# A seventh unit's long rows turned by way of DRAM, and a new hand-laid order

## Chip, cores and metric

The kernel runs on one core of one Trainium2 chip. The metric is device time in microseconds (us): the median of three runs was 361.75 us (361.44 to 361.85).

## What is computed

Two attention layers follow each other, in float32. The first is attention over a window of 128 positions with 4 sink positions (batch 4, 8 heads, 768 positions, head width 64); its output, seen as `x` with 512 columns, enters a mixture of four attention experts, of which each position takes the best two.

```python
scores = where(is_sink | in_window, scale * q @ k.T, -1e9)
x      = softmax(scores) @ v                      # per batch and head, then heads side by side
logits = x @ w_gate;  w = softmax of the two largest logits
for e in range(4):                                # causal attention of expert e, width 64
    a   = softmax(causal(scale * (x @ wq[e]) @ (x @ wk[e]).T))
    out += weight_of(e) * (a @ (x @ wv[e]) @ wo[e])
```

## The kernel before

The work is cut into 24 units. A unit of the first layer is one batch and one pair of heads; a unit of the second layer is one batch and one pair of experts. Units are named by three digits, batch, pair, layer: unit 001 is batch 0, expert pair 0, second layer. They come in the order of `ORD` and `LAST` (L1944, L1945): the four head pairs of batch 0, then 110, 100, **001**, 120, 130, 011, 210 and so on; 301 and 311 are the last.

A unit of the second layer (`second`, L1828) projects `x` to queries and keys, then works six blocks of 128 rows (`wide_rows`, L1566). Row block i sees i+1 key blocks. Scores go to PSUM (L1385), DVE takes the mask and the minimum (L1602), ACT the exponential and its sum (L1610), POOL and DVE make the factor, ACT or POOL scale the row (L1256, L1258). The values can only be applied (L1424) once the row is transposed, and there are two ways to do that:

- **On PE** (`transposed`, L1463, and `turned`, L1453): every 128 by 128 block is transposed by two matmuls against a unit matrix (L1457) into PSUM, and ACT or DVE carry it back to SBUF (`pt`, L1247 and L1249). Rows 4 and 5 are cut in two parts (`SPLIT`, L1942), each with its own transposing step and its own step of applying values.
- **By way of DRAM** (`by_way_of_dram`, L1536): the row is scaled into a tile `u`, DVE transposes the 32 by 32 squares within it (two instructions, L1547), one DMA writes `u` to the DRAM tile `there` (L1550), four DMAs read it back with the squares exchanged (L1554), and PE applies the values straight from `u` in one step (L1424). PE transposes nothing. There are three `u` tiles and four `there` tiles (L1043).

`AWAY` (L1940) says which rows of which units go by way of DRAM: rows 3, 4 and 5 of the units 011, 101, 111, 201, 211 and 301. A unit with such rows also takes its row pairs from the last to the first (`groups[::-1]` in `wide_rows`). Units 001 and 311 have none.

The order of every instruction on every engine is fixed while the program is built. `Plan.emit` (L907) simulates the engines with a cost per step and picks, again and again, the next step. On PE the choice goes by one key (L958): the step's priority, plus a charge `STAY` (and a term with `BULK`) where the step needs another shape of the PE array than the last, plus `HURRY` per 100 ns of waiting. The dictionary `NUDGE` adds a number of its own to the priority of single steps and kinds of steps (3,033 entries), and `ONLY` fixes for 396 steps which engine takes them. Shapes of the array are FULL (128 by 128), "cols" (128 rows by 64 columns: applying values), "rows" (64 by 128: scores and PE transposes) and "quad" (64 by 64: banded scores). Where PE would have nothing to do in the first 130 us, dummy matmuls are put in (L1057). On the chip each engine runs its list in order and waits on semaphores.

Of the kernel before, what the change touches and what calls it, by code (L numbers as in the profile page):

```python
# [34 lines left out]
for other in ("ROWS", "FULL", "cols", "rows"):  # L35
# [10 lines left out]
    "busy_PE": 2.7, " ": -0.4, " busy_PE": 50.2, " busy_PE 0": 4.1, "sink_values_DVE": 20.3, " sink_values_DVE": 16.0,  # L46
    " sink_values_DVE 0": -121.8, "load_SP": -59.6, " load_SP": 21.7, " load_SP 0": 11.3, "again_SP": 5.1,
    " again_SP": 21.0, " again_SP 0": -23.8, "sink_values_ACT": -3.5, " sink_values_ACT": -29.8, " sink_values_ACT 0": 49.4,
    "sink_values_POOL": 12.3, " sink_values_POOL": 5.5, " sink_values_POOL 0": -91.6, "sink_values_SP": 4.4,
    " sink_values_SP": 35.9, " sink_values_SP 0": -24.8, "load_SPACT": 0.1, " load_SPACT": 12.9, " load_SPACT 0": -10.8,  # L50
# [768 lines left out]
    "311 store_SPACT 3": SP, "311 fn_DVEACT 20": ACT, "311 fn_DVEACT 21": DVE, "311 store_SPACT 5": SP,  # L819
}  # L820

HURRY = 71.82
STAY = 104.82
BULK = -0.39
# [1197 lines left out]
```

## Time and profile before

| | before |
|---|---|
| median of 3 runs | 361.75 us |
| the profiled execution's own time | 361.39 us |
| its span, first to last instruction | 359.7 us |
| granted TensorE clock, mean | 0.998 of full |
| matmuls / DVE / ACT / POOL busy | 98% / 81% / 77% / 51% of the span |

The profile is one execution. Busy time of an engine is the union of its instructions; matmuls overlap and their ends are modelled, so their start times are the safer reading. "PEld" is the loading of weights into the array, which runs beside matmuls. In the chain of waits the trace is followed back from the last instruction to whatever released it.

### The profile page before, as it was taken

To read this page: it belongs to the slowest core of one execution; us is meant where nothing else is said; L and a number is where in the kernel's file an instruction comes from. 1 tells how busy PE (TensorE), PEld (TensorE's weight loads), DVE (VectorE), ACT (ScalarE), POOL (GpSimd) and SP (SyncE) were. 2 spreads that over 40 slices of the span, in tenths; PEclk is the share of its full clock that TensorE was granted. 3 is DMA by queue.
4 is the path that set the end of the run, shared out by engine and by line. 5 is a ranking of instruction groups with operands and counts; after the bars stand their busy time and mean duration, and the time that the engine had idled before them with its cause. 6 is when DMAs were issued, how large, how long until landed. Compare 5 with 4: busy or idle time off the path is not lost.

```text
span 359.7 us, 13333 instructions
## 1 busy us (share of the span) xinstructions
PE 351.2 (98%) x4822; PEld 307.1 (85%) x4822; DVE 290.6 (81%) x1263; ACT 278.7 (77%) x985; POOL 183.2 (51%) x432
## 2 busy tenths in 40 slices
PE   8989999999999999999999999999999999999995
PEld 7877789998888889978888888978898889988884
DVE  4899989599979979649799987489699875587951
ACT  2899999299998899758898977489899956056931
POOL 4298999778276764334646550153558600150420
PEclk9999999999999999999999999999999999999999
DMA  7877787943550798329787595029800463059313
GB/s 200 214 178 144 149 165 142 173 77 84 92 87 3 234 263 156 58 88 307 207 159 124 162 283 122 11 87 352 218 7 4 145 223 76 14 201 300 103 58 118
DMA packets 130849, 52.05 MB, mean 145 GB/s; under 512 B 109728, under 2 KB 125088, under 8 KB 130784
## 3 DMA queue, kind: packets, MB, share of 16 engines
q1 hardware_dynamic: 118336, 46.23, 52.0%
q10 hardware_dynamic: 12448, 4.98, 5.3%
...
## 4 chain that ended last, share of the span: by engine, by line
PE 80%; ACT 7%; DMA 4%; DVE 3%; POOL 3%; issue 2%; SPq 0%; ACTq 0%; POOLq 0%; DVEq 0%
PE b L1424 19%; PE b L1839 17%; PE b L1913 10%; PE b L1866 9%; PE b L1385 8%; PE b L1457 7%; PE b L1398 5%; PE b L1380 2%; DMA u<-there 2%; ACT p L1610 2%; PE b L1924 1%; ACT p L1740 1%; DMA there<-u 1%; PE b L1428 1%; DMA vn<-in_v_dram 1%
## 5 line engine op out<-in xcount | busy, mean ns | idle before, releaser
L1610 ACT ACTIVATE p<-p,st 128x256 f32<-128x256 f32 (+5 forms) x96 | 63.6, 665 | 9.8 <-DVE st L1602 9.6
L1740 ACT ACTIVATE p<-p,st 128x132 f32<-128x132 f32 x128 | 51.3, 406 | 3.2 <-DVE st L1736 3.1
L1602 DVE CUSTOM_DVE_ANT_0 p<-b,cmask 128x384 f32<-128x384 f32 (+3 forms) x96 | 45.7, 502 | 1.9 <-PE b L1385 1.5
L1247 ACT ACTIVATE pt<-b 128x256 f32<-128x256 f32 (+3 forms) x101 | 38.5, 419 | 7.5 <-PE b L1457 7.3
L1385 PE MATMUL b<-ks,qs 64*128 64x384 f32 (+3 forms) x384 | 42.2, 338 | 0.0
L1424 PE MATMUL b<-pt,vn 128*64 128x128 f32 x448 | 39.0, 280 | 0.3 <-ACT pt L1247 0.3
L1866 PE MATMUL b<-wvh,x 128*128 128x260 f32 x192 | 36.9, 285 | 0.0
L1440 POOL TENSOR_TENSOR st<-st 128x2 f32<-128x2 f32 (+1 forms) x47 | 9.3, 197 | 52.7 <-ACT p L1610 36.1
L1457 PE MATMUL b<-ident,p 64*128 64x64 f32 x760 | 36.0, 226 | 0.0
L1457 PEld LDWEIGHTS b<-ident,p 64*128 64x128 f32 x760 | 30.4, 138 | 5.4 <-issue 2.5
L1385 PEld LDWEIGHTS b<-ks,qs 64*128 64x128 f32 x384 | 31.6, 186 | 3.3 <-issue 0.7
L1839 PE MATMUL b<-x,wqh 128*128 128x256 f32 (+1 forms) x128 | 32.8, 343 | 0.0
L1839 PE MATMUL b<-x,wkh 128*128 128x256 f32 (+1 forms) x128 | 32.5, 340 | 0.0
L1913 PE MATMUL b<-woh,y 128*128 128x512 f32 x96 | 32.2, 402 | 0.0
L1753 POOL TENSOR_TENSOR p<-p,st 128x528 f32<-128x528 f32 x23 | 24.5, 1066 | 15.0 <-DVE st L1445 10.8
L1547 DVE STREAM_TRANSPOSE u<-u 128x640 f32<-128x640 f32 (+2 forms) x36 | 28.5, 824 | 4.0 <-ACT u L1256 3.7
L1736 DVE CUSTOM_DVE_ANT_0 p<-b,pair_mask 128x132 f32<-128x132 f32 x128 | 31.6, 286 | 0.1
L1679 ACT ACTIVATE p<-p,st 128x256 f32<-128x256 f32 (+1 forms) x64 | 29.1, 460 | 2.9 <-DVE st L1674 2.8
L1866 PEld LDWEIGHTS b<-wvh,x 128*128 128x128 f32 x192 | 30.4, 188 | 0.7 <-issue 0.3
L1249 DVE COPY pt<-b 128x256 f32<-128x256 f32 (+3 forms) x63 | 27.5, 453 | 2.6 <-PE b L1457 2.5
L1424 PEld LDWEIGHTS b<-pt,vn 128*64 128x64 f32 x448 | 25.1, 136 | 4.6 <-issue 1.7
L1866 PE MATMUL b<-wvl,x 128*128 128x260 f32 x96 | 27.1, 282 | 0.0
...
## 6 DMA issues: line engine op xcount, KB each, us to landing
vn<-in_v_dram SPq DMA_DIRECT2D x24, 192.0 KB, 3.3
...
there<-u SPq DMA_DIRECT2D x6, 768.0 KB, 4.8
u<-there SPq DMA_DIRECT2D x24, 192.0 KB, 4.6
...
```

The lines of the kernel that those rows point to most:

```text
L1247: nc.scalar.activation(dst(), src(), AF.Copy)
L1385: nc.tensor.matmul(o, self.qs.t[hs, a, qs], keys(hs, b), start=n == 0, stop=n == 2)
L1424: nc.tensor.matmul(o[e * 64:e * 64 + 64], lhs, rhs, start=e not in self.begun, stop=last and self.done == len(self.steps))
L1457: nc.tensor.transpose(t[g].t[:, n, :], x[gs], ident[gs, gs])
L1602: nc.vector.tensor_tensor_reduce(out=one(e)[:, cs], in0=s2[e].t[:, :(c1 - c0) * 128], in1=mask(c0, c1), scale=times, scalar=st.t[:, 3, es] ...
L1610: nc.scalar.activation(x, x, AF.Exp, bias=st.t[:, 0, es], scale=-1.0, accum_out=st.t[:, 1, es])
L1679: nc.scalar.activation(x, x, AF.Exp, bias=st.t[:, 0, n:n + 1], scale=-1.0, accum_out=st.t[:, 1, n:n + 1])
L1736: nc.vector.tensor_tensor_reduce(out=p.t[:, n, :], in0=s2[e].t[:, 248 * r:248 * r + SW], in1=pair_mask, scale=-scale, scalar=BIG, op0=OP.a ...
L1740: nc.scalar.activation(p.t[:, n, :], p.t[:, n, :], AF.Exp, bias=st.t[:, 0, n:n + 1], scale=-1.0, accum_out=st.t[:, 1, n:n + 1])
L1839: nc.tensor.matmul(t.t, w[a][:, c, es], X[b, c].t[:, x, cs], start=c == 0 and m == 0, stop=c == NCH - 1 and m == 2)
L1866: nc.tensor.matmul(t.t[:, :VW], X[b, c].t[:, a, qs], W["wv"][w][:, c, :], start=c == 0 and n == 0, stop=c == NCH - 1 and n == 2)
L1913: nc.tensor.matmul(t.t, Y[b, c].t[:, a, qs], W["wo"][w][:, c, :], start=c == 0 and n == 0, stop=c == EP - 1 and n == 2)
```

## The change

Unit 001 is added to `AWAY`: its rows 3, 4 and 5 go by way of DRAM, and its row pairs are taken from the last to the first. The three constants of PE's key change, and `NUDGE` and `ONLY` are replaced throughout (3,069 and 430 entries; of the 2,942 nudges that both have, three keep their value). Nothing else differs.

```diff
-    "001 tr_PE 4": 0.5, "001 fn_DVEACT 14": 26.1, "001 fn_DVEACT 15": 30.9, "001 all_of_PE 3": -1.9, "001 tr_PE 5": 23.7,
...
+    "001 turn_DVE 3": 82.4, "001 by_way_of_dram_SP 1": 186.4, "001 back_SP 1": -0.2, "001 av_PE 1": -12.8,
...
-HURRY = 71.82
-STAY = 104.82
-BULK = -0.39
+HURRY = 80.98
+STAY = 193.1
+BULK = -55.63
...
-    AWAY, MOVE = {u: (3,4,5) for u in ((0, 1), (1, 0), (1, 1), (2, 0), (2, 1), (3, 0))}, 250
+    AWAY, MOVE = {u: (3,4,5) for u in ((0, 0), (0, 1), (1, 0), (1, 1), (2, 0), (2, 1), (3, 0))}, 250
```

## Rows read from the trace of the kernel before

**Rows 1.** The page's table of busy time: microseconds, share of the span, instructions.
```profile
PE 351.2 (98%) x4822; PEld 307.1 (85%) x4822; DVE 290.6 (81%) x1263; ACT 278.7 (77%) x985; POOL 183.2 (51%) x432
```

**Rows 2.** Who PE's matmuls waited for over the whole span: microseconds in total, times, longest; five rows of 0.6 us or less follow. Asked for the stretch from 60 us to the end alone, the view has the second of these rows and no other.
```profile
PE b L1924 <- DVE lanes L1110: 1.1, 1, 1.1
PE b L1424 <- DMA u<-there: 0.8, 1, 0.8
PE b L1398 <- POOL kx L1322: 0.7, 1, 0.7
```

**Rows 3.** Busy time by stretch: the stretch in us, its length, then PE, PEld, DVE, ACT and POOL busy (instructions), granted clock, DMA share, GB/s.
```profile
0.00:20.00 20.00, 18.38 (x402) 15.70 (x404) 14.19 (x84) 11.18 (x45) 8.56 (x32) 1.00 0.83 215
...
80.00:100.00 20.00, 20.00 (x342) 17.48 (x341) 19.50 (x98) 19.69 (x69) 10.69 (x23) 1.00 0.50 92
100.00:120.00 20.00, 19.97 (x268) 17.50 (x268) 17.88 (x61) 18.02 (x66) 15.59 (x37) 1.00 0.36 82
120.00:140.00 20.00, 20.00 (x292) 17.65 (x289) 17.74 (x88) 18.32 (x76) 11.65 (x29) 1.00 0.88 217
```

**Rows 4.** PE's instructions in order of time while unit 001 works its rows: start us, us, then line, operation, tiles, shape and count.
```profile
74.18 0.60 PE L1385 MATMUL b<-ks,qs 64*128 64x256 f32 x6
...
86.60 0.71 PE L1457 MATMUL b<-ident,p 64*128 64x64 f32 x16
87.15 0.87 PE L1380 MATMUL b<-kx,qn 64*128 64x128 f32 x8
87.86 0.53 PE L1457 MATMUL b<-ident,p 64*128 64x64 f32 x12
88.32 1.58 PE L1398 MATMUL b<-kx,qn 64*64 64x196 f32 x48
89.83 0.59 PE L1457 MATMUL b<-ident,p 64*128 64x64 f32 x12
90.25 0.87 PE L1380 MATMUL b<-kx,qn 64*128 64x128 f32 x8
91.06 2.40 PE L1424 MATMUL b<-pt,v 128*64 128x128 f32 x40
93.39 1.41 PE L1457 MATMUL b<-ident,p 64*128 64x64 f32 x32
```

**Rows 5.** Pieces of the chain of waits, followed back from the end of the stretch 70 to 120 us: start us, us, engine, tile, line, count. L1457 transposes, L1424 applies values.
```profile
78.12 0.46 PE b L1457 x10
...
91.12 2.33 PE b L1424 x40
...
107.00 1.17 PE b L1457 x32
110.16 0.81 PE b L1424 x12
```

**Rows 6.** Groups of instructions by form over the whole span (count, busy us, mean ns of one): the squares' transposes on DVE, the copies out of PSUM, the scaling of rows.
```profile
L1547 DVE STREAM_TRANSPOSE u<-u 128x768 f32<-128x768 f32 x12 | 11.1, 951 | 0.9 <-ACT u L1256 0.9
L1547 DVE STREAM_TRANSPOSE u<-u 128x640 f32<-128x640 f32 x12 | 9.7, 828 | 2.5 <-ACT u L1256 2.5
L1547 DVE STREAM_TRANSPOSE u<-u 128x512 f32<-128x512 f32 x12 | 8.1, 692 | 0.6 <-POOL u L1258 0.3 <-ACT u L1256 0.3
...
L1247 ACT ACTIVATE pt<-b 128x384 f32<-128x384 f32 x37 | 17.0, 496 | 5.1 <-PE b L1457 4.9
L1247 ACT ACTIVATE pt<-b 128x512 f32<-128x512 f32 x3 | 1.7, 596 | 0.0
...
L1258 POOL TENSOR_SCALAR u<-p,st 128x640 f32<-128x640 f32 x11 | 8.8, 800 | 0.1
L1258 POOL TENSOR_SCALAR p<-p,st 128x640 f32<-128x640 f32 x2 | 1.6, 800 | 0.2
```

**Rows 7.** DMA issues by tile: issuing queue, count, KB each, median us from issue to landing.
```profile
there<-u SPq DMA_DIRECT2D x6, 768.0 KB, 4.8
u<-there SPq DMA_DIRECT2D x24, 192.0 KB, 4.6
...
there<-u SPq DMA_DIRECT2D x6, 512.0 KB, 5.1
u<-there SPq DMA_DIRECT2D x24, 128.0 KB, 4.7
```

**Rows 8.** The tile `there`: its DMA instructions (ns to issue one, min/median/max, first and last start), and the time to landing of all of them.
```profile
L1554 SPq DMA_DIRECT2D u<-there x72: 302/430/1563, 123.4 to 332.1; - x72
L1550 SPq DMA_DIRECT2D there<-u x18: 326/344/1114, 116.9 to 324.0; - x18
...
DMA to landing us min/median/max: 2.5/4.5/7.1
```

**Rows 9.** The chain of waits around 205 us, where it leaves PE: start us, us, what.
```profile
206.24 4.16 DMA there<-u
...
211.84 7.06 DMA u<-there
...
219.04 1.53 PE b L1424 x24
```

**Rows 10.** SP's issues in the stretch 80 to 120 us, in order of time: the first and the last of the four lines that load queries and keys of units to come (sixteen DMAs in all).
```profile
89.98 2.04 SPq L1804 DMA_DIRECT2D qn<-in_q_dram  x4
...
101.51 2.54 SPq L1804 DMA_DIRECT2D kn<-in_k_dram  x4
```

More of the change, by code (lines that the diff above doesn't have):

```diff
@@ L45 @@
 NUDGE = {
[L46 to L50, printed above, removed]
@@ L817 @@
[L817 to L824 removed]
+    " load_SPACT 1": SP, " load_SPACT 2": ACT, " load_SPACT 4": ACT, " load_SPACT 6": SP, "000 load_SPACT 0": SP,
+    "000 load_SPACT 1": SP, "000 load_SPACT 3": SP, "000 load_SPACT 4": SP, "000 fn_DVEACT 1": DVE, "000 fn_DVEACT 6": ACT,
@@ new lines @@
+    "000 fn_DVEACT 7": DVE, "000 total_DVEPOOL 0": DVE, "000 norm_POOLACT 0": ACT, "000 norm_POOLACT 1": POOL,
+    "000 fn_DVEACT 8": ACT, "000 fn_DVEACT 9": ACT, "000 norm_POOLACT 2": ACT, "000 fn_DVEACT 10": DVE,
+    "000 fn_DVEACT 11": ACT, "000 fn_DVEACT 12": DVE, "000 fn_DVEACT 13": ACT, "000 fn_DVEACT 14": ACT,
+    "000 fn_DVEACT 15": DVE, "000 fn_DVEACT 16": ACT, "010 load_SPACT 0": SP, "010 load_SPACT 1": SP,
+    "010 fn_DVEACT 0": DVE, "010 fn_DVEACT 1": DVE, "010 fn_DVEACT 2": ACT, "010 fn_DVEACT 3": DVE, "010 fn_DVEACT 4": DVE,
@@ new lines @@
+    "010 fn_DVEACT 5": ACT, "010 fn_DVEACT 6": DVE, "010 fn_DVEACT 7": DVE, "010 norm_POOLACT 0": ACT,
+    "010 norm_POOLACT 1": POOL, "010 fn_DVEACT 8": ACT, "010 fn_DVEACT 9": DVE, "010 norm_POOLACT 2": ACT,
+    "010 fn_DVEACT 10": DVE, "010 fn_DVEACT 11": DVE, "010 fn_DVEACT 12": DVE, "010 fn_DVEACT 13": ACT,
+    "010 total_DVEPOOL 2": DVE, "010 norm_POOLACT 3": POOL, "010 fn_DVEACT 14": ACT, "010 fn_DVEACT 15": DVE,
+    "010 fn_DVEACT 16": ACT, "010 fn_DVEACT 17": DVE, "020 load_SPACT 0": SP, "020 load_SPACT 1": SP,
@@ new lines @@
+    "030 fn_DVEACT 7": ACT, "030 total_DVEPOOL 0": DVE, "030 norm_POOLACT 1": POOL, "030 fn_DVEACT 8": DVE,
+    "030 total_DVEPOOL 1": POOL, "030 norm_POOLACT 2": ACT, "030 fn_DVEACT 11": DVE, "030 total_DVEPOOL 2": POOL,
+    "030 fn_DVEACT 14": DVE, "110 load_SPACT 0": SP, "110 load_SPACT 2": SP, "110 total_DVEPOOL 0": DVE,
+    "110 norm_POOLACT 0": POOL, "110 norm_POOLACT 1": ACT, "110 fn_DVEACT 4": ACT, "110 norm_POOLACT 3": ACT,
+    "110 fn_DVEACT 8": ACT, "110 fn_DVEACT 9": DVE, "100 load_SPACT 1": SP, "100 load_SPACT 2": SP,
@@ new lines @@
+    "100 total_DVEPOOL 0": DVE, "100 norm_POOLACT 0": ACT, "100 fn_DVEACT 1": ACT, "100 total_DVEPOOL 1": POOL,
+    "100 fn_DVEACT 2": DVE, "100 fn_DVEACT 3": ACT, "100 fn_DVEACT 4": ACT, "100 total_DVEPOOL 2": POOL,
+    "100 norm_POOLACT 3": POOL, "100 fn_DVEACT 8": DVE, "100 fn_DVEACT 9": ACT, "001 fn_DVEACT 0": DVE,
+    "001 fn_DVEACT 1": ACT, "001 fn_DVEACT 5": DVE, "001 norm_POOLACT 0": POOL, "001 total_DVEPOOL 1": POOL,
+    "001 norm_POOLACT 2": ACT, "001 norm_POOLACT 3": POOL, "001 total_DVEPOOL 2": DVE, "001 norm_POOLACT 4": POOL,
@@ new lines @@
+    "001 fn_DVEACT 6": ACT, "001 total_DVEPOOL 3": POOL, "001 norm_POOLACT 7": POOL, "001 total_DVEPOOL 4": DVE,
+    "001 norm_POOLACT 8": POOL, "001 norm_POOLACT 9": POOL, "001 fn_DVEACT 8": DVE, "001 fn_DVEACT 9": ACT,
+    "001 norm_POOLACT 11": ACT, "001 fn_DVEACT 10": ACT, "120 load_SPACT 1": SP, "120 load_SPACT 2": SP,
+    "120 norm_POOLACT 0": ACT, "120 norm_POOLACT 1": POOL, "120 fn_DVEACT 1": ACT, "120 norm_POOLACT 2": POOL,
+    "120 fn_DVEACT 2": ACT, "120 fn_DVEACT 4": DVE, "120 fn_DVEACT 5": DVE, "120 total_DVEPOOL 2": POOL,
@@ new lines @@
+    "120 fn_DVEACT 6": DVE, "120 fn_DVEACT 8": DVE, "120 fn_DVEACT 9": DVE, "130 load_SPACT 0": SP, "130 load_SPACT 1": SP,
+    "130 total_DVEPOOL 0": DVE, "130 norm_POOLACT 0": ACT, "130 norm_POOLACT 1": ACT, "130 fn_DVEACT 1": ACT,
+    "130 norm_POOLACT 2": POOL, "130 fn_DVEACT 2": ACT, "130 fn_DVEACT 4": ACT, "130 fn_DVEACT 5": ACT,
+    "130 total_DVEPOOL 2": DVE, "130 fn_DVEACT 6": ACT, "130 fn_DVEACT 8": ACT, "130 fn_DVEACT 9": ACT,
+    "011 total_DVEPOOL 0": POOL, "011 norm_POOLACT 0": POOL, "011 total_DVEPOOL 1": POOL, "011 norm_POOLACT 2": POOL,
@@ new lines @@
+    "011 norm_POOLACT 3": POOL, "011 total_DVEPOOL 2": POOL, "011 norm_POOLACT 4": POOL, "011 norm_POOLACT 5": POOL,
+    "011 fn_DVEACT 0": ACT, "011 total_DVEPOOL 3": POOL, "011 norm_POOLACT 6": POOL, "011 total_DVEPOOL 4": POOL,
+    "011 norm_POOLACT 9": POOL, "011 fn_DVEACT 2": ACT, "011 norm_POOLACT 10": ACT, "011 norm_POOLACT 11": POOL,
+    "011 fn_DVEACT 5": DVE, "011 store_SPACT 0": ACT, "011 fn_DVEACT 7": DVE, "011 store_SPACT 1": SP,
+    "011 fn_DVEACT 8": ACT, "011 fn_DVEACT 9": DVE, "011 store_SPACT 3": SP, "011 fn_DVEACT 10": DVE,
@@ new lines @@
+    "011 store_SPACT 5": ACT, "210 load_SPACT 1": SP, "210 load_SPACT 2": SP, "210 norm_POOLACT 0": POOL,
+    "210 norm_POOLACT 1": POOL, "210 fn_DVEACT 0": ACT, "210 total_DVEPOOL 1": POOL, "210 norm_POOLACT 2": POOL,
+    "210 norm_POOLACT 3": ACT, "210 fn_DVEACT 6": DVE, "210 fn_DVEACT 7": DVE, "210 fn_DVEACT 8": ACT,
+    "200 load_SPACT 0": SP, "200 load_SPACT 2": SP, "200 norm_POOLACT 0": POOL, "200 norm_POOLACT 1": POOL,
+    "200 fn_DVEACT 0": DVE, "200 fn_DVEACT 1": ACT, "200 total_DVEPOOL 1": POOL, "200 norm_POOLACT 2": ACT,
@@ new lines @@
+    "101 norm_POOLACT 10": POOL, "101 norm_POOLACT 11": POOL, "101 fn_DVEACT 10": ACT, "101 fn_DVEACT 11": ACT,
+    "220 load_SPACT 0": SP, "220 total_DVEPOOL 0": DVE, "220 norm_POOLACT 1": POOL, "220 fn_DVEACT 0": DVE,
+    "220 fn_DVEACT 1": ACT, "220 total_DVEPOOL 1": POOL, "220 fn_DVEACT 2": DVE, "220 fn_DVEACT 3": ACT,
+    "220 fn_DVEACT 4": DVE, "220 fn_DVEACT 5": DVE, "220 norm_POOLACT 3": ACT, "220 fn_DVEACT 8": ACT,
+    "220 fn_DVEACT 9": ACT, "230 load_SPACT 1": SP, "230 fn_DVEACT 0": ACT, "230 fn_DVEACT 1": ACT,
@@ new lines @@
+    "230 total_DVEPOOL 1": POOL, "230 fn_DVEACT 2": ACT, "230 fn_DVEACT 3": ACT, "230 fn_DVEACT 4": ACT,
+    "230 fn_DVEACT 5": DVE, "230 total_DVEPOOL 2": POOL, "230 norm_POOLACT 3": POOL, "230 fn_DVEACT 7": ACT,
+    "230 fn_DVEACT 8": ACT, "111 total_DVEPOOL 0": POOL, "111 norm_POOLACT 0": POOL, "111 norm_POOLACT 1": POOL,
+    "111 total_DVEPOOL 1": DVE, "111 norm_POOLACT 3": POOL, "111 norm_POOLACT 4": POOL, "111 total_DVEPOOL 3": DVE,
+    "111 norm_POOLACT 6": ACT, "111 norm_POOLACT 7": POOL, "111 total_DVEPOOL 4": POOL, "111 norm_POOLACT 8": ACT,
@@ new lines @@
+    "111 fn_DVEACT 2": ACT, "111 fn_DVEACT 3": DVE, "111 total_DVEPOOL 5": DVE, "111 norm_POOLACT 11": POOL,
+    "111 fn_DVEACT 4": ACT, "111 fn_DVEACT 5": ACT, "111 store_SPACT 0": SP, "111 fn_DVEACT 7": ACT,
+    "111 store_SPACT 1": SP, "111 fn_DVEACT 8": DVE, "111 store_SPACT 2": SP, "111 store_SPACT 3": SP,
+    "111 fn_DVEACT 10": ACT, "111 store_SPACT 4": SP, "111 fn_DVEACT 11": ACT, "111 store_SPACT 5": ACT,
+    "300 load_SPACT 0": SP, "300 load_SPACT 1": SP, "300 total_DVEPOOL 0": POOL, "300 norm_POOLACT 0": POOL,
@@ new lines @@
+    "201 fn_DVEACT 6": ACT, "201 norm_POOLACT 7": ACT, "201 total_DVEPOOL 4": DVE, "201 norm_POOLACT 9": POOL,
+    "201 fn_DVEACT 8": ACT, "201 fn_DVEACT 9": ACT, "201 total_DVEPOOL 5": DVE, "201 norm_POOLACT 10": ACT,
+    "201 norm_POOLACT 11": ACT, "201 fn_DVEACT 10": ACT, "310 load_SPACT 0": SP, "310 total_DVEPOOL 0": DVE,
+    "310 norm_POOLACT 0": POOL, "310 total_DVEPOOL 1": POOL, "310 norm_POOLACT 2": POOL, "310 fn_DVEACT 2": DVE,
+    "310 fn_DVEACT 3": ACT, "310 fn_DVEACT 4": ACT, "310 fn_DVEACT 5": DVE, "310 total_DVEPOOL 2": DVE,
@@ new lines @@
+    "310 norm_POOLACT 3": POOL, "310 fn_DVEACT 6": DVE, "310 fn_DVEACT 8": DVE, "320 load_SPACT 0": SP,
+    "320 load_SPACT 1": SP, "320 norm_POOLACT 0": POOL, "320 fn_DVEACT 0": ACT, "320 fn_DVEACT 1": ACT,
+    "320 total_DVEPOOL 1": POOL, "320 norm_POOLACT 2": POOL, "320 fn_DVEACT 3": DVE, "320 fn_DVEACT 4": ACT,
+    "320 norm_POOLACT 3": POOL, "320 fn_DVEACT 6": DVE, "320 fn_DVEACT 7": ACT, "320 fn_DVEACT 8": DVE,
+    "320 fn_DVEACT 9": DVE, "330 load_SPACT 1": SP, "330 total_DVEPOOL 0": POOL, "330 norm_POOLACT 1": ACT,
@@ new lines @@
+    "330 fn_DVEACT 0": ACT, "330 fn_DVEACT 1": DVE, "330 total_DVEPOOL 1": DVE, "330 norm_POOLACT 2": POOL,
+    "330 fn_DVEACT 2": DVE, "330 fn_DVEACT 3": ACT, "330 fn_DVEACT 4": DVE, "330 fn_DVEACT 5": DVE,
+    "330 norm_POOLACT 3": POOL, "330 fn_DVEACT 7": ACT, "330 fn_DVEACT 8": ACT, "330 fn_DVEACT 9": ACT,
+    "211 norm_POOLACT 1": POOL, "211 total_DVEPOOL 1": DVE, "211 norm_POOLACT 2": POOL, "211 norm_POOLACT 3": POOL,
+    "211 total_DVEPOOL 2": DVE, "211 norm_POOLACT 4": ACT, "211 norm_POOLACT 5": POOL, "211 fn_DVEACT 0": DVE,
@@ new lines @@
+    "211 fn_DVEACT 1": ACT, "211 norm_POOLACT 7": POOL, "211 total_DVEPOOL 4": POOL, "211 norm_POOLACT 8": POOL,
+    "211 norm_POOLACT 9": ACT, "211 fn_DVEACT 2": ACT, "211 total_DVEPOOL 5": POOL, "211 norm_POOLACT 11": POOL,
+    "211 fn_DVEACT 4": ACT, "211 fn_DVEACT 5": ACT, "211 fn_DVEACT 6": ACT, "211 fn_DVEACT 7": ACT, "211 store_SPACT 1": SP,
+    "211 fn_DVEACT 11": ACT, "211 store_SPACT 5": SP, "301 fn_DVEACT 0": DVE, "301 fn_DVEACT 1": ACT,
+    "301 fn_DVEACT 2": DVE, "301 fn_DVEACT 3": ACT, "301 fn_DVEACT 4": ACT, "301 total_DVEPOOL 0": DVE,
@@ new lines @@
+    "311 norm_POOLACT 0": POOL, "311 fn_DVEACT 0": DVE, "311 fn_DVEACT 1": DVE, "311 total_DVEPOOL 1": DVE,
+    "311 norm_POOLACT 2": POOL, "311 norm_POOLACT 3": POOL, "311 fn_DVEACT 2": ACT, "311 fn_DVEACT 3": DVE,
+    "311 fn_DVEACT 5": ACT, "311 total_DVEPOOL 3": POOL, "311 fn_DVEACT 6": DVE, "311 total_DVEPOOL 4": DVE,
+    "311 norm_POOLACT 8": POOL, "311 fn_DVEACT 8": ACT, "311 fn_DVEACT 9": DVE, "311 fn_DVEACT 10": ACT,
+    "311 fn_DVEACT 11": DVE, "311 total_DVEPOOL 5": DVE, "311 norm_POOLACT 11": POOL, "311 fn_DVEACT 12": ACT,
@@ L825 @@
+    "311 fn_DVEACT 13": DVE, "311 fn_DVEACT 15": ACT, "311 fn_DVEACT 16": DVE, "311 store_SPACT 0": SP,
+    "311 store_SPACT 1": ACT, "311 store_SPACT 2": SP, "311 fn_DVEACT 19": ACT, "311 store_SPACT 3": SP,
+    "311 fn_DVEACT 20": ACT, "311 store_SPACT 4": ACT, "311 fn_DVEACT 21": ACT, "311 store_SPACT 5": SP,
+}
+HURRY = 80.98
+STAY = 193.1
+BULK = -55.63
 FILL_COST, FILL_KEEP, FILL_END = 220.0, 0.0, 130000.0
```

132 lines of the change are left out of this document (34 added, 98 removed), and 1339 rows, old and new, of the table NUDGE.

## Prediction

> **What bounds the kernel.** I read the table of busy time first: PE 98% [rows 1]. Since the ends of matmuls are modelled, that alone proves nothing, so I went on to what PE waited for. In the whole span that is a handful of waits near 1 us or below, and from 60 us on a single one, 0.8 us for a read back from DRAM [rows 2]. The stretches agree: 18.38 us of matmuls in the first 20 us, then 20.00, 19.97 and 20.00 of 20 from 80 to 140 us, at full clock [rows 3]. So from 60 us to the end PE's list of instructions is the time. What leaves this list shortens the kernel one for one, as long as no other engine takes its place. The nearest is DVE: 19.50 and 17.88 us busy of 20 in the two stretches in which unit 001 works its rows, ACT 19.69 and 18.02 [rows 3].
>
> The Trainium skill's page "Perfetto Trace Analysis", section "Identifying the Most-Contended Engine", warns that matmul busy time is a poor measure of headroom and wants the busy share of weight loads instead; that is 85% here. By it 15% of the engine would be free and the sum below would be nothing (a rival). The waits speak against it: PE hardly waits for anyone.
>
> **What leaves PE.** Row 3 has 4 key blocks, row 4 has 5, row 5 has 6; each block is two heads by two halves, so 16 + 20 + 24 = 60 transposes go. The chain's pieces give their price without the modelled ends [rows 5]: 10 transposes take 0.46 us and 32 take 1.17, so one is (1.17 - 0.46) / 22 = 0.032 us, and a run of them costs 0.46 - 0.32 = 0.14 us besides, the turn of the array to another shape. 60 x 0.032 = **1.94 us**.
>
> The 60 stand in five steps (one for row 3, two each for rows 4 and 5). In time order they are the runs of 16, 12, 12 and 32, the last holding other transposes too [rows 4]. I let four runs disappear: 4 x 0.14 = **0.55 us**. Bounds: none, if other transposes move in, and about 1.4 us, if all five go and each also joins its two neighbours into one run.
>
> Applying the values is the same number of matmuls from `u` as from `pt`. But five steps become three. A run of 12 takes 0.81 us and one of 40 takes 2.33 [rows 5], so a matmul is 0.054 us and the run itself 0.16. Two runs fewer would be 0.32 us; half of it, as such runs are often joined already: **0.16 us** (bounds 0 and 0.32). Together 2.65 us, between 1.9 and 3.7.
>
> **What it adds elsewhere, and why I cost it at nothing.**
> - DVE gets two transposes of squares per row: 2 x (0.69 + 0.83 + 0.95) = 4.94 us [rows 6]. It loses its share of ten copies out of PSUM, which at ACT's means would be 0.60 us for 512 columns and 0.50 for 384; most of them are ACT's today, so ACT gains about 4 us and DVE pays nearly all of its 4.94. From 80 to 120 us DVE has 40 - 37.4 = 2.6 us free [rows 3]. That is not enough unless the order gives ACT other copies, which it can: every such copy may go to either engine, and the new `ONLY` redistributes them. The cover is thus ACT's freed time. Bounds: 0, and 4.94 - 2.6 = 2.3 us. I take 0, since together the two engines gain as much as they lose.
> - Scaling a row into `u` costs what scaling it in place costs: 800 ns each for 640 columns [rows 6].
> - SP issues three writes and twelve reads: 3 x 0.34 + 12 x 0.43 = 6.2 us [rows 8], and the reads wait on SP until the write has landed, 3.4 to 5.1 us by size at the median [rows 7]. Behind them stand loads of later units [rows 10]: sixteen DMAs from 90 to 104 us, which now share the queue. DVE needs them for its turns; they are prefetched, and a few us of delay is covered. If not, DVE stands still, and this falls into the first rival.
> - Data: 768 + 640 + 512 KB out and the same back, 3.84 MB more in a stretch that moves 92 and 82 GB/s at DMA shares of 0.50 and 0.36. The stretch after it, with detours of its own, carries 217 GB/s at 0.88 [rows 3]; the extra 96 GB/s over 40 us fits.
> - The unit's row pairs come from the last to the first, so its first scores need all projections. Before, its first long scores began at 74.18 us, behind the projections as well [rows 4]; nothing is lost.
>
> Here a rule of the Trainium skill speaks against the change. "DMA: Bandwidth & Descriptors", section "Rules for kernel authors", puts transposing by a plain DMA with a rearranged pattern at 19 times the cost of the hardware's DMA transpose. The rows do not show such a penalty: a read back of 192 KB lands in 4.6 us at the median, a plain write of 768 KB in 4.8 [rows 7]. Were the four reads of row 5 to take 19 times the 4.8, some 91 us by my estimate, PE would wait for most of it.
>
> **What the new order brings.** Every other instruction may move, and the trace shows none of that, so I bound it. To the good: the one late read back costs PE 0.8 us [rows 2], from a write of 4.16 us and a read of 7.06 us in sequence [rows 9]; and turns of the array. From 86.60 to 93.39 us PE begins nine runs of one shape [rows 4], at 0.14 to 0.16 us each. In the key the charge for a turn rises from 104.82 / 71.82 = 1.46 to 193.1 / 80.98 = 2.38 hundred ns of waiting, so fewer turns are chosen where nudges do not decide. If over some 200 us of such stretches one run in twelve went, that is about 200 x 9 / 6.8 / 12 x 0.15 = 3.3 us. To the bad: the same number of turns more, 3.3 us, or new waits. I take the value nearest to a row, the 0.8 us wait and one turn of 0.16: **1.0 us** gained, ends -4.1 and +3.3.
>
> **The sum.** 361.39 us of the profiled execution - 2.65 - 1.0 = 357.7. The median stands 0.36 us above that execution, so 358.1 us for the median. The good end is 361.75 - 3.7 - 4.1 = 354.0; the bad side is the rivals'.
>
> **Rivals.**
> - *DVE takes PE's place* between 80 and 120 us. For it: the 2.3 us that do not fit. Against it: ACT's freed time, and that PE has work of other units to do meanwhile. Price: 2.3 us and the order's 1.0 not had: 358.1 + 3.3 = 361.4 us, at worst; a milder form lies near 360.
> - *The reads back land after PE has come to their matmuls* (slower). PE's list is fixed; where the data is not there, everything behind waits. Before, one of 18 rows was late, by 0.8 us [rows 2]. After, 21 rows stand at new places, and landings spread from 2.5 to 7.1 us around 4.5 [rows 8]. If a third, seven rows, came late by as much: 7 x 0.85 = 6.0 us, so 361.75 - 2.65 + 6.0 = 365.1 us. It decides from the fifth late row on (4.3 x 0.85 = 3.65 us, all that I forecast). Against it: 17 of 18 were in time, and the new detours lie where DMA has most room.
> - *PE is not the bound*: the weight loads' 85% are the truth, the transposes ran beside other work, and nothing changes: 361.7 us. Against it: waits after 60 us are 0.8 us in all, and the pieces of the chain grow linearly with the count.
> - *The order saves far more*, over 4.1 us of turns and waits: below 354.0 us.
>
> That the change doesn't do what it says I exclude: `second` looks up exactly this key in `AWAY`.
>
> **Chances.** Forecast 0.61; DVE 0.15; late reads 0.16; not the bound 0.03; far more 0.05. About 0.2% (0.7 us) is what a measurement of this kernel can tell from no change. Faster by more than that: 0.61 + 0.05 + two thirds of DVE's 0.15 = 0.76. Within it: the other third, "not the bound", and a little of the late reads: 0.09. Slower: 0.15. The range is 354.0 to 362.0 us; it leaves out the 0.05 below and nearly all of the late reads above.
>
> **What would show it.** In the changed kernel's profile: 700 transposes in the group at L1457 where there were 760, 42 transposes of squares where there were 36, 21 writes to `there`; in PE's waits still no more than about 1 us after 60 us; DVE under 20 us of 20 in 80 to 120 us. If the forecast is wrong, PE's busy time falls while waits for `u` or DVE grow by as much (second and first rival), or PE's runs become more and shorter. Wrong by size would be an order that saves whole microseconds of turns.

## The result, and the profile after

The changed kernel took **364.32 us** at the median (360.78 to 367.67, 20 runs) against 361.44 us of the kernel before on the same chip: the ratio is 1.007 [1.0048, 1.0093], so it is slower by 0.7%, where 358.1 us and a gain were forecast. The ratio leaves out executions in the slower state, two of these twenty. Its profiled execution took 362.49 us, with a span of 360.8. Lines of the changed kernel are 22 higher than before: transposes on PE L1479, values L1446, squares on DVE L1569, loads L1826.

The table of busy time, against [rows 1]:

```profile
PE 352.1 (98%) x4802; PEld 307.9 (85%) x4802; DVE 292.0 (81%) x1272; ACT 271.3 (75%) x952; POOL 190.6 (53%) x449
```

20 matmuls are missing, not 60: the sixty transposes went, and there are 40 more dummy matmuls (118, before 78), nearly all of them in the first 40 us. DVE gained 1.4 us, ACT lost 7.4, and POOL gained 7.4: work did move between them.

The groups of instructions by form, against [rows 5, 6], and the tile `there`, against [rows 8]. The change does what it says:

```profile
L1479 PE MATMUL b<-ident,p 64*128 64x64 f32 x700 | 34.4, 226 | 0.0
...
L1569 DVE STREAM_TRANSPOSE u<-u 128x768 f32<-128x768 f32 x14 | 13.1, 958 | 0.2 <-POOL u L1280 0.2
L1569 DVE STREAM_TRANSPOSE u<-u 128x640 f32<-128x640 f32 x14 | 11.4, 830 | 1.1 <-ACT u L1278 1.1
L1569 DVE STREAM_TRANSPOSE u<-u 128x512 f32<-128x512 f32 x14 | 9.6, 696 | 0.5 <-POOL u L1280 0.4
```

```profile
L1576 SPq DMA_DIRECT2D u<-there x84: 302/431/1447, 87.8 to 333.0; - x84
L1572 SPq DMA_DIRECT2D there<-u x21: 319/343/348, 83.8 to 324.9; - x21
...
DMA to landing us min/median/max: 2.4/4.4/7.2
```

Who PE waited for in the changed kernel (total us, times, longest), against [rows 2]:

```profile
PE b L1450 <- DVE ks L1332: 1.2, 1, 1.2
PE b L1946 <- DVE lanes L1132: 1.1, 1, 1.1
PE b L1446 <- DMA u<-there: 1.1, 1, 1.1
```

The middle one stands at the beginning, as before. The other two are new. The stretches, in the columns of [rows 3], show where:

```profile
80.00:100.00 20.00, 20.00 (x240) 16.62 (x240) 18.52 (x82) 19.56 (x74) 14.65 (x33) 1.00 0.73 197
100.00:120.00 20.00, 18.93 (x333) 16.95 (x324) 19.50 (x85) 17.07 (x61) 12.86 (x29) 1.00 0.82 169
160.00:180.00 20.00, 20.00 (x223) 16.95 (x223) 16.02 (x61) 13.18 (x48) 9.45 (x22) 1.00 0.88 262
180.00:200.00 20.00, 18.55 (x324) 16.26 (x320) 19.21 (x84) 18.55 (x71) 14.05 (x34) 1.00 0.63 118
```

PE is 1.07 us short in the stretch 100 to 120, and 1.45 us in 180 to 200. The first is the read back of unit 001's row 5, the new detour. The second comes from ACT. In ACT's order of time (start, us, engine, line, what) the four query loads of unit 330 are issued at 171.27 us, and ACT does nothing else for 5 us:

```profile
171.24 0.22 ACT L1269 ACTIVATE sk<-b 64x64 fp32r<-64x64 f32 x1
171.27 5.13 ACTq L1826 DMA_DIRECT2D qn<-in_q_dram  x4
176.45 0.41 ACT L1762 ACTIVATE p<-p,st 128x132 f32<-128x132 f32 x1 [4.99 <-DVE kx L1377]
```

In the kernel before, ACT issued the same four loads at 221.77 us in 0.34 + 1.69 us:

```profile
221.77 0.34 ACTq L1804 DMA_DIRECT2D qn<-in_q_dram  x1
222.16 1.69 ACTq L1804 DMA_DIRECT2D qn<-in_q_dram  x3
```

In the changed kernel ACT's later work shifts, the turn of the queries and the split of the keys on DVE come late, and PE waits at 182 us.

### The profile page after: what moved, and what is told of

Same layout as the page of the kernel before. It is cut to its first block, busy times and chain, and to the rows that moved or that the text cites. A ratio compares the mean times of both kernels' runs of the same rounds, so it can differ in the third digit from the quotient of the medians.

```text
span 360.8 us, 13315 instructions
## 1 busy us (share of the span) xinstructions
PE 352.1 (98%) x4802; PEld 307.9 (85%) x4802; DVE 292.0 (81%) x1272; ACT 271.3 (75%) x952; POOL 190.6 (53%) x449
## 4 chain that ended last, share of the span: by engine, by line
PE 74%; DVE 10%; DMA 5%; SPq 4%; ACT 3%; issue 2%; POOL 1%; DVEq 0%; POOLq 0%; ACTq 0%
PE b L1446 18%; PE b L1861 13%; PE b L1407 9%; PE b L1888 8%; PE b L1935 7%; PE b L1479 7%; PE b L1420 5%; DMA u<-there 2%; PE b L1402 2%; SPq L1826 2%; PE b L1359 1%; DVE kx L1377 1%; PE b L1946 1%; PE b L1450 1%; DVE u L1569 1%
## 5 line engine op out<-in xcount | busy, mean ns | idle before, releaser
L1632 ACT ACTIVATE p<-p,st 128x768 f32<-128x768 f32 (+5 forms) x96 | 63.7, 666 | 9.2 <-DVE st L1624 9.0
L1407 PE MATMUL b<-ks,qs 64*128 64x384 f32 (+3 forms) x384 | 43.5, 340 | 0.2 <-DVE ks L1332 0.2
L1269 ACT ACTIVATE pt<-b 128x256 f32<-128x256 f32 (+3 forms) x96 | 36.5, 416 | 7.2 <-PE b L1479 4.8
L1446 PE MATMUL b<-pt,vn 128*64 128x128 f32 x448 | 39.2, 279 | 0.0
L1569 DVE STREAM_TRANSPOSE u<-u 128x640 f32<-128x640 f32 (+2 forms) x42 | 34.0, 828 | 1.7 <-ACT u L1278 1.1
L1479 PE MATMUL b<-ident,p 64*128 64x64 f32 x700 | 34.4, 226 | 0.0
L1462 POOL TENSOR_TENSOR st<-st 128x2 f32<-128x2 f32 (+1 forms) x53 | 10.5, 199 | 43.5 <-ACT p L1632 24.1
L1479 PEld LDWEIGHTS b<-ident,p 64*128 64x128 f32 x700 | 28.8, 138 | 5.2 <-issue 2.0
L1861 PE MATMUL b<-x,wkh 128*128 128x512 f32 (+1 forms) x128 | 32.3, 340 | 0.0
L1446 PEld LDWEIGHTS b<-pt,vn 128*64 128x64 f32 x448 | 25.5, 136 | 2.9 <-DVE st L1624 0.3
L1471 POOL TENSOR_TENSOR st<-st,gate 128x2 f32<-128x2 f32 x48 | 9.2, 197 | 35.4 <-DVE st L1467 29.5
L1446 PE MATMUL b<-u,v 128*64 128x128 f32 x420 | 26.2, 274 | 1.1 <-DMA u<-there 1.1
```

Source lines behind the costliest of these rows:

```text
L1269: nc.scalar.activation(dst(), src(), AF.Copy)
L1407: nc.tensor.matmul(o, self.qs.t[hs, a, qs], keys(hs, b), start=n == 0, stop=n == 2)
L1446: nc.tensor.matmul(o[e * 64:e * 64 + 64], lhs, rhs, start=e not in self.begun, stop=last and self.done == len(self.steps))
L1479: nc.tensor.transpose(t[g].t[:, n, :], x[gs], ident[gs, gs])
L1569: nc.vector.transpose(x(), x())
L1632: nc.scalar.activation(x, x, AF.Exp, bias=st.t[:, 0, es], scale=-1.0, accum_out=st.t[:, 1, es])
```

## Experiments

All kernels with a list EDITS replay the planned order of the kernel they start from, with single steps moved or given to another queue just before the instructions are made; nothing else differs, and lines behind the list are 10 higher again. Ratios are to the kernel before, on the same chip.

**1. Unedited, once more** (`again`).

> The changed kernel once more, unedited, for a second trace and more clocks. In its twenty runs the ones with a mean clock of 0.998 or above took 361.4 to 362.5 us (one of 1.0: 360.8) and those of 0.993 took 362.8 to 365.3. Theory W (waits): PE stands still at two new places (1.07 us at 103 us for row 5's read back of the new detour, 1.19 + 0.23 us at 182 us for key copies that ACT made late, because four loads held its queue for 5.13 us), and in most runs the standing still also costs the clock: this run is between 362 and 366 us, and if its mean clock is below 0.998, the trace shows a stretch at 1.2 GHz right behind one of the two places. Rival O (order): the clock falls somewhere else, in a stretch where PE waits for nothing or in the first 60 us.

363.86 us, 1.0082 [1.0054, 1.0111], as theory W had it. Row 5's wait at 103 us is absent this time; the one at 182 us is larger. PE's instructions in order of time there:

```profile
182.53 0.44 PE L1450 MATMUL b<-sk,vs 64*128 64x128 f32 x2 [2.27 <-DVE ks L1332]
183.19 2.31 PE L1420 MATMUL b<-kx,qn 64*64 64x196 f32 x48 [0.22 <-DVE qs L1332]
185.43 2.19 PE L1446 MATMUL b<-u,v 128*64 128x128 f32 x20
```

The run of 20 takes 2.19 us here, where it took 1.31 us in the changed kernel's first profile. The stretch view (granted clock third from the end) shows why: behind the wait the clock is 0.56 of full, nearly all of it the lower of its two levels (1.2 GHz). In the first profile, after a wait of 1.19 us, it stayed at 1.00.

```profile
184.26:187.68 3.42, 3.42 (x49) 3.09 (x42) 3.42 (x20) 2.64 (x12) 0.70 (x1) 0.56 0.39 94
```

So in this execution one late step costs twice: 2.3 to 2.5 us of waiting, and at least 0.9 us of slow matmuls. Of the chain of waits, the pieces that lead there:

```profile
170.63 4.38 DMA qn<-in_q_dram
175.00 0.02 issue
175.03 0.02 ACTq L1826
175.04 0.04 issue
175.08 5.93 DMA qn<-in_q_dram
...
181.13 1.04 DVE qn L1377 x2
182.17 0.31 DVE ks L1332
```

The fourth load is issued when the *first* has landed (170.63 + 4.38 = 175.01).

**2. The order at the two new waits** (`sp_first`, `act_free`, `both`, `turn_late`, `act_late`).

```diff
 # sp_first: the reads back of row 5 ahead of unit 200's loads on SP
+EDITS = [("before", "001 back_SP 1", "200 load_SPACT 0")]
 # turn_late: unit 330's two query turns behind a key turn on DVE
+EDITS = [("before", "330 turn_DVE 0", "330 turn_DVE 1"), ("before", "330 turn_DVE 2", "330 turn_DVE 1")]
 # act_free: turn_late, and 330's query loads to SP, behind its key loads
+  ("engine", "330 load_SPACT 0", "SP"), ("behind", "330 load_SPACT 0", "330 load_SPACT 1")
 # act_late: turn_late, and 330's query loads to SP, behind unit 320's key loads
+  ("engine", "330 load_SPACT 0", "SP"), ("behind", "330 load_SPACT 0", "320 load_SPACT 1")
```

> The changed kernel with one move on SP: the four reads of row 5 of the new detour are issued ahead of the four query loads that stood before them, all else as it was. W: the reads land some 2 to 3.5 us earlier, PE's wait of 1.07 us at 103 us goes, and the median falls by 1 us (by 2 to 3, if this is the place that costs the clock). O: something else is late next (the loads now come 2 us later and DVE turns them at 99.7 us), and the median stays within 0.5 us of the changed kernel's.

371.01 us, 1.0274 [1.0253, 1.0295]: missed by far. SP now stands at the reads until the write has landed, and loads behind them are late; PE waits 3.9 us for keys alone. Both this and the next edit together (`both`) gave 372.48 us, where 358.5 to 360 were expected.

> The changed kernel with the four query loads of unit 330 issued by SP, behind that unit's key loads, instead of by ACT at 171 us, and the two DVE turns that need them put just ahead of the unit's key turns (215 us in the plan), long before they are used. W: ACT does not stand for 5 us at 171 to 176 us, PE's waits of 1.19 and 0.23 us at 182 us go, and the median falls by 1.4 us, by 2 to 3.5 if this is the place that costs the clock. O: within 0.5 us of the changed kernel.

365.73 us, 1.0115 [1.0081, 1.0149]: missed as well. The wait for keys is gone, but the loads now stand on SP ahead of a detour's reads, and PE waits 4.5 us for those.

> The changed kernel with two DVE instructions moved: the turns of unit 330's queries, which stand in DVE's list at 180 us right behind the landing of their load, now stand just ahead of that unit's key turns at about 220 us (the unit is worked at 260 us). Theory D: these two turns make DVE wait for a load that crowded DMA queues deliver late; the key copies behind them come late, PE stands still for 1.2 to 2.3 us at 182 us, and the clock then falls to 1.2 GHz for 3.4 us. It expects the wait at 182 us gone or under 0.5 us, the low clock in the middle of the run rare, and the median 361.5 to 362.2 us (changed kernel 363.9). Rival A: it is ACT, held for about 5 us by the issue of the same load, that makes the copies late; then a wait of 1 us or more stays and the median is within 0.7 us of 363.9.

364.2 us, 1.0072 [1.0055, 1.0089]: as the changed kernel, with a wait of 0.92 us for keys and the low clock behind it. The order of DVE's turns is not the cause.

```profile
PE b L1460 <- DVE ks L1342: 0.9, 1, 0.9
```

> As before, and the four query loads of unit 330 are issued by SP behind the key loads of unit 320 (about 194 us) instead of by ACT at 171 us. D: within 0.5 us of the run with the two turns moved alone. A: 1 us or more below it, with ACT busy through 171 to 176 us.

**360.93 us, 0.9991 [0.9975, 1.0007]**, where `turn_late`, which differs from it by the place and the queue of one load step alone, had 1.0072. PE's waits in its profile:

```profile
PE b L1956 <- DVE lanes L1142: 1.1, 1, 1.1
PE b L1456 <- DMA u<-there: 0.8, 2, 0.5
PE b L1430 <- ACT qn L1279: 0.3, 1, 0.3
```

That is A's result: one load step costs 0.8%, some 2.9 us. What is left of the change, detour and order together, is within the measurement of no change.

**3. Is it ACT's queue, or the place?** (`act_same`, `act_before`)

```diff
 # act_same: as act_late, but the loads stay on ACT
-  ("engine", "330 load_SPACT 0", "SP"),
 # act_before: the kernel before, 330's query loads (on ACT) moved some 15 us ahead
+EDITS = [("behind", "330 load_SPACT 0", "111 back_SP 0")]
```

> The changed kernel with the four query loads of unit 330 at the late place (behind the key loads of unit 320, with the two query turns late), but issued from ACT instead of SP. At the old place the fourth of them was issued only when the first had landed (170.63 + 4.38 = 175.01, issued at 175.08 us), in a stretch with a detour's reads and an output store in flight. Theory A1, the place decides (transfers in flight, whose landing semaphores are still taken): at the late place few transfers are in flight, the four issues take about 2 us on ACT as in the kernel before (0.34 + 1.69 us), and the time is that of the loads on SP there, 360.9 us (360.4 to 361.8). Rival A2, ACT's queue decides wherever the loads stand: ACT stands for 4 to 5 us again, PE waits over 1 us for keys or rows of other units behind it, and the time is 362.5 us or more.

364.29 us, 1.01 [1.0079, 1.0122]: both theories missed. ACT issued the four in 0.93 + 1.14 us, as A1 said, and the time was A2's. PE waited 2.2 us for a read back and 1.5 us for ACT (the longest 1.2).

> The kernel before with one step moved: the four query loads of unit 330, which ACT issues at 221.8 us, go to just behind the first reads back of unit 111's detour (about 207 us), into a stretch with two more writes and eight more reads. Nothing else changes; no detour of unit 001. If a load step on ACT among a detour's transfers is harmful by itself: ACT stands for 4 to 5 us, a wait of 1 us or more of PE for work of ACT or DVE appears between 208 and 222 us, and the time is 1 to 4 us above the kernel before: 362.3 to 365.3 us. Rival, it was only the changed order that had no slack at that place: ACT stands as long, but PE's waits stay below 1 us and the time is within 0.7 us of the kernel before.

363.45 us, 1.0067 [1.0047, 1.0087]: one load step moved in the kernel *before* costs as much as the whole change. But ACT did not stand (0.34 + 1.72 us). SP did. Who PE waited for longest, who SP's issues waited for between 195 and 212 us (total us, times, longest), and the detour's first writes in SP's order of time:

```profile
PE b L1434 <- DMA u<-there: 2.0, 1, 2.0
```

```profile
SPq L1560 <- DMA vn<-in_v_dram: 8.4, 1, 8.4
```

```profile
207.35 1.51 SPq L1560 DMA_DIRECT2D there<-u  x2
```

In the kernel before, the first write left at 200.15. Here its data was complete at 200.48 us, and it waited for the landing of a *value load*, with which it has nothing in common. What ties these runs together is in the trace's issue records. Every transfer signals its landing through a semaphore; the program has eight for that (101 and 103 to 109 in the changed kernel), and hands them out in turn to all its 300 transfers, whichever queue issues them; the order on both queues fits this without exception. A transfer whose semaphore was last given to another is issued only when that one has landed: the trace of the changed kernel records the landing of the one before for 146 transfers, and none of the 146 was issued ahead of it. The records of the changed kernel (issue time, queue, landing semaphore, transfer; Scalar is ACT):

```
170.50 Sync   103 u<-there
171.03 Sync   104 out_dram<-o
171.27 Scalar 108 qn<-in_q_dram
171.66 Scalar 101 qn<-in_q_dram
172.93 Scalar 105 qn<-in_q_dram
174.98 Sync   106 there<-u
175.41 Sync   107 u<-there
175.84 Sync   109 u<-there
176.09 Scalar 108 qn<-in_q_dram
```

The first and the fourth load share 108: five of SP's transfers come between them in the program's count. In `act_before` the detour's first write got 106, which a value load on ACT had (issued 204.07, landed 3.20 us later, at 207.27; the write went at 207.35). In `act_same` the second of a detour's four reads got 109, that of a value load issued on ACT at 183.66, and went at 186.57 with two more behind it; in `act_late` only the fourth read got 109. So ACT's queue as such is not the cause, nor the place as such: a load that ACT issues late holds whichever transfer stands eight further on, on either queue.

The Trainium skill's page "DMA: Bandwidth & Descriptors", section "Why a DMA increments its semaphore by 16 and not by 1", gives a reason for such a wait: with two transfers in flight on one semaphore, a wait for the first can pass too early, so it wants one semaphore per transfer in flight. No run here shows a wait that passed too early.

What the wait costs, the rows here show: 3.2 us lay between the third and the fourth load on ACT (172.93 to 176.09; 0.5 us in the kernel before), and SP's write stood 6.9 us (200.48 to 207.35).

**4. The same wait in the kernel before** (`vn_before`). [rows 2] and [rows 9] had such a wait already. DVE's and SP's order of time in the kernel before, for the second write of unit 111's detour:

```profile
202.62 0.97 DVE L1547 STREAM_TRANSPOSE u<-u 128x768 f32<-128x768 f32 x1
```

```profile
200.15 6.44 SPq L1550 DMA_DIRECT2D there<-u  x2
206.68 2.43 SPq L1554 DMA_DIRECT2D u<-there  x4
```

```diff
+EDITS = [("engine", "320 load_SPACT 2", "SP"), ("behind", "320 load_SPACT 2", "111 by_way_of_dram_SP 1")]
```

> The kernel before with one step changed: the two value loads of unit 320 leave ACT's queue (203.24 us) for SP's, right behind the second write of unit 111's detour. In the kernel before that write was complete in SBUF at 202.62 + 0.97 = 203.59 us, yet was issued at 206.24, when the first of these loads had landed (203.24 + 2.92 = 206.16): both use the landing semaphore 104, which goes to every eighth transfer of the program, and a transfer is issued only when the one before it on its semaphore has landed. Theory S (the shared landing semaphore holds the write): the write now leaves within 1 us of 203.6, its reads land before PE needs them, PE's one wait after 60 us (0.8 us for the read back) goes, and the time falls by 0.5 to 1.0 us. Rival (the write was late for its data or for SP's other work): it leaves at 206 as before and nothing changes, within 0.3 us.

The write left at 203.54 us: the two writes' issue now lasts 3.85 us, not 6.44, and PE's wait for `u` is gone.

```profile
200.03 3.85 SPq L1560 DMA_DIRECT2D there<-u  x2
203.97 1.54 SPq L1810 DMA_DIRECT2D vn<-in_v_dram  x2
```

```profile
PE b L1934 <- DVE lanes L1120: 1.1, 1, 1.1
PE b L1408 <- POOL kx L1332: 0.4, 1, 0.4
PE b L1434 <- ACT pt L1257: 0.3, 1, 0.3
```

The mechanism is shown. The time, 360.91 us, 0.9992 [0.9979, 1.0004], has the expected sign, but at 0.3 to 0.5 us it is smaller than the expected 0.5 to 1.0 and not told apart from no change.

**5. Moves that changed more than the queue** (`act_step`, `vn_soon`; `vn_late` is like the latter, with the value loads behind the last reads back: 368.44 us where 360.1 to 360.6 were expected, as PE waits 4.5 us for the value loads themselves).

```diff
 # act_step: the changed kernel, loads still on ACT, one step earlier
+EDITS = [("before", "330 load_SPACT 0", "101 back_SP 0")]
 # vn_soon: act_late, and unit 230's value loads to SP
+  ("engine", "230 load_SPACT 2", "SP"), ("behind", "230 load_SPACT 2", "101 back_SP 1")
```

> The changed kernel with the four query loads of unit 330 still issued from ACT, but before the first reads back of unit 101's detour instead of behind them. In the changed kernel the fourth of them carried the same landing semaphore (108) as the first, since eight transfers of both queues lie between them, and was issued at 176.09 us or 175.08, when the first had landed. Here seven lie between the first and the fourth, and the fourth follows on its semaphore a read back that is issued at about the same time. Theory S: the wait is now for that read, so ACT stands 2 to 5 us according to its landing, PE's wait for keys at 182 us is smaller but not gone, and the time lies between 361.0 and 363.5 us. Rival A2 (loads on ACT are bad by themselves): as the changed kernel, 363.5 to 364.5 us.

370.99 us, 1.0269 [1.0237, 1.0301]. Moved ahead, the load overtakes the last matmuls that read the tile's former unit, so these now wait for it and use the wrong unit's rows: PE stands 5.8 us for the load itself. It says nothing on either theory.

> The kernel that gave 360.9 us (query loads of unit 330 on SP, late), with the two value loads of unit 230 on SP as well, but right behind the second reads back of unit 101's detour, some 6 us earlier than ACT issued them, where their tile has long been free. No transfer on ACT is then between the detour's. Theory S (the eight shared landing semaphores): the last reads back of 101 are issued together by about 183 us instead of the last at 186.4, the values come early, PE has no wait for u in 180 to 200 us, and the time is 360.0 to 360.7 us. Rival (that wait was covered, or SP's queue becomes too long): 360.8 us or more.

360.72 us, 0.9984 [0.9968, 1.0000]. Here too some matmuls of the tile's former unit read the new values, so it is no version to keep. The reads of 101's last row went out together (183.86 to 185.37 us), and PE's waits for `u` there are gone, as theory S has it; the one left, 1.3 us at 104 us, is row 5 of unit 001 again. A version that beats both kernels and computes the same was not found.

**6. What sixty transposes are worth** (`no_turn2`, `light_dve`, `no_turn_dve`, `no_copy`, `no_both`; and the detour in the old order, `away_fwd`).

```diff
 # no_turn2: the kernel before, without unit 001's transposes on PE
-            for m in range(n):
+            for m in range(0 if gone else n):
 # no_copy: besides, its copies out of PSUM cut to one column
-  pt.t[:, :, 64 * g:64 * g + 64]
+  pt.t[:, :1 if gone else n, 64 * g:64 * g + (1 if gone else 64)]
 # light_dve, no_turn_dve, no_both: no masked copies of units 120 and 130 on DVE,
 # in the kernel before, in no_turn2 and in no_copy
+                if light:
+                    return
```

> The kernel before with its order as it was, but the 60 PE transposes of unit 001's rows 3, 4 and 5 left out (everything around them stays, so those rows are wrong; the ten dummy matmuls at the start write to other banks). It measures the term of the sum by itself, without detour and without a new order. The prediction's sum gives 2.5 us less (1.94 for the transposes and 0.55 for their turns), so about 358.9 us against 361.4, bounds 1.9 to 3.3. Rival N (PE not the bound): less than 0.7 us.

360.38 us, 0.9975 [0.9959, 0.999]: 0.9 us, not the 2.5 of the two terms. PE's waits have a new first row, in a stretch in which it had none, and from 90 to 100 us DVE and ACT are as full as in the kernel before (its line stands last):

```profile
PE b L1398 <- DVE st L1737: 1.2, 1, 1.2
```

```profile
80.00:90.00 10.00, 9.99 (x164) 8.37 (x160) 9.74 (x49) 9.68 (x25) 7.51 (x17) 1.00 0.35 78
90.00:100.00 10.00, 8.79 (x116) 7.51 (x114) 9.71 (x52) 10.00 (x46) 2.60 (x6) 1.00 0.64 103
```

```profile
90.00:100.00 10.00, 10.00 (x160) 8.62 (x159) 9.83 (x55) 10.00 (x43) 2.32 (x5) 1.00 0.63 102
```

> The kernel before without DVE's eight masked copies of units 120 and 130 (8 x 0.42 = 3.2 us of DVE between 88 and 100 us; left out, so scores of the sinks stay where they were). All of PE's work is there. If PE is the bound there, as its 20.00 us of 20 say, DVE's relief alone brings nothing: within 0.4 us of the kernel before. If DVE were the bound already, up to 2 to 3 us would be gained.

361.21 us, 1.0004 [0.999, 1.0019]: with PE's work all there, DVE is no limit.

> The kernel before without the 60 transposes of unit 001 on PE and without DVE's eight masked copies of units 120 and 130 (both left out). Without the transposes alone the time fell by only 0.9 us (ratio 0.9975), with PE waiting 1.2 us for DVE. If DVE took PE's place there: that wait goes and the full 2 to 2.6 us of the transposes come out, 358.7 to 359.4 us. Rival, the transposes are worth only some 1 us to PE, as they ran beside other matmuls: 360.2 to 360.6 us, like the run without the transposes alone.

360.2 us, 0.9982 [0.9966, 0.9999]. That is the rival's time. From 90 to 100 us DVE has room (7.19 of 10 us), ACT is at 10.00, and PE waits as long.

> The kernel before without the 60 transposes of unit 001 on PE and with its ten copies out of PSUM cut to one column each (both left out in effect), as the detour takes both away; nothing is put in their place. Without the transposes alone 0.9 us came out, PE waiting 1.2 us for DVE; with DVE lightened by 3.2 us besides it was no more, ACT being busy for 10.00 of 10 us between 90 and 100 us. Theory E (DVE and ACT were both at their limits, and the ten copies are what has to leave with the transposes): PE's wait goes and 1.8 to 2.6 us come out, 358.6 to 359.4 us. Rival (the transposes ran beside other matmuls, and are worth no more than 1 us): 360.0 to 360.5 us.

359.95 us, 0.9957 [0.9943, 0.9971], short of what theory E expected: ACT has room (9.10 of 10 us), DVE not (9.60), PE waits 1.3 us.

> The kernel before without the 60 transposes of unit 001, with its ten copies out of PSUM cut to one column, and without the eight masked copies of units 120 and 130 on DVE (all left out in effect): DVE and ACT both relieved between 80 and 100 us. Each relief alone left PE waiting 1.2 to 1.3 us there. Theory E (DVE and ACT are each at their limit there, so that only both reliefs free PE): the wait goes and 2.2 to 2.8 us come out, 358.5 to 359.2 us. Rival (a chain of latencies sets the time there, whatever DVE and ACT have to do): the wait stays above 1 us and the time at 359.8 to 360.3 us.

**359.4 us, 0.9941 [0.992, 0.9961]**: 2.1 us come out (1.4 to 2.9), and PE's wait falls to 0.9 us.

```profile
PE b L1929 <- DVE lanes L1110: 1.1, 1, 1.1
PE b L1398 <- DVE st L1741: 0.9, 1, 0.9
```

```profile
80.00:90.00 10.00, 10.00 (x176) 8.88 (x174) 9.66 (x46) 9.46 (x29) 8.84 (x19) 1.00 0.36 81
90.00:100.00 10.00, 9.12 (x125) 7.68 (x120) 7.47 (x49) 9.98 (x51) 3.24 (x6) 1.00 0.58 93
```

DVE's relief alone gave nothing back (0.9982 against 0.9975 without it), that of the copies perhaps 0.6 us (0.9957; the intervals overlap), both together 1.2 us. The last run lies between its two expectations, and ACT is still at 9.98 of 10 us in it, so theory E is supported but not shown; that a part of the wait is latency, as its chain runs through short steps of ACT, POOL and DVE in turn, is not shown either.

What the transposes are worth on PE itself can be added up from the traces: from start to next start, without waits and dummy matmuls, PE's work is 341.4 to 342.4 us in `before`, `vn_before` and `light_dve`, and 339.6 to 340.3 us in the four runs without the transposes. That is about 2 us, the 1.94 of the first term alone.

> The kernel before with unit 001 added to the rows that go by way of DRAM, its old nudges and constants, and its row pairs in the old direction (first to last), so that the old nudges still meet the steps they were made for. Structure without the new order. If the detour's saving of 2.65 us comes without an order made for it: 358.8 to 360 us. If an order is needed (theory O): 362 or more, with PE waiting for reads back or for DVE between 80 and 120 us.

377.42 us, 1.0443 [1.0425, 1.0461]: the detour dropped into the old order, with the old row order, waits for POOL's rows (3.6 us) and ACT's copies. It needs an order of its own.

## Why the prediction was wrong, point by point

- **What bounds the kernel**: right as far as it went. With PE's work in place, 3.2 us less on DVE changed nothing (`light_dve`). But "what leaves this list shortens the kernel one for one, as long as no other engine takes its place" needs room on the engines beside PE, and in the kernel before's order there was none: 0.9 us of about 2 came out (`no_turn2`).
- **What leaves PE, 2.65 us**: the count was right (700 transposes, 42 of squares, 21 writes), and so was the 1.94 us of the transposes: PE's own work shrank by about 2 us. The 0.55 us for four runs was not there. From 86.60 to 93.39 us [rows 4] has eight lines, not nine, and only five runs of one array shape, as transposes and scores share the shape 64 by 128. A change of shape does cost the 0.14 us that was read, but `no_turn2` has only one change fewer (156, before 157). The Trainium skill's rule by the weight loads' share, by which, as the prediction reads it, nothing would come out, is not borne out by the 2.1 us (1.4 to 2.9) of `no_both`.
- **"What the new order brings: 1.0 us gained"**: this step failed, and it decided the sign. It was read from three constants and the shape of the array, to which no trace had a row for waits. The order put one step of four loads on ACT at 171 us, between another detour's transfers: 2.9 us lost by `turn_late` against `act_late`. The turns brought nothing either way: there are 152 changes of array shape, before 157, and those with no wait beside them, 148 in each kernel, cost 20.7 us, before 20.6. The text had a bad end of 3.3 us for the order, priced as turns, with "or new waits" beside it; the 2.9 us lie within it. But the range did not carry this end: its bad side was left to the rivals, at 362.0 us.
- **"Why I cost it at nothing"**: not safe, but not shown to be what failed. [rows 3] had DVE at 19.50 and ACT at 19.69 of 20 us; a stretch whose PE work shrinks by 2 us has to fit theirs into less time as well, and in the kernel before's order it did not (`no_turn2`). The new order met this in part: of DVE's 4.94 us only 1.4 appear in its total. With the harmful load step away (`act_late`, 360.9 us) PE's work is 339.6 us, as short as without the transposes, and its only wait after 60 us is 0.8 us for reads back, none for DVE. So that run has nearly the time of the first rival's milder form, "near 360", without its sign. What its trace has more is dummy matmuls and waits in the first 60 us: 12.1 to 13.2 us in six traces of the changed order, 11.1 to 12.0 in eight of the old one. No run tests whether the detour, by way of the planner, is what put them there.
- **SP's queue**: I costed issue times and the wait of reads for their write. I did not see that a transfer also waits for the transfer eight places before it, on either queue, though [rows 9] had it: the write at 206.24 us was complete at 203.59.
- **The second rival**, reads back that land late (365.1 us), has nearly the right time for another reason. Landings were as forecast (2.4/4.4/7.2 us) and one row was late by 1.1 us in one of two profiles, far from five.
- **The Trainium skill's factor of 19** for a transposing plain DMA was rightly set aside, for a read that exchanges whole squares which DVE has already transposed: reads of 192 KB land in 4.1 us at the median after the change, 4.6 in [rows 7].
- **Signs**: PE's waits after 60 us add up to more than 2 us, which the text named as the sign of the first two rivals; the releasers were key copies and one read.

Not settled: the time of the changed kernel from run to run, 360.78 to 367.67 us, fits a wait that is sometimes followed by a stretch at the lower clock; how often each occurs, and when the clock falls, the profiles don't show. Nor was the new order without the detour tried.
